# q and k of the fourth token chunk by seven block products, and a new plan for the splitting of the MLP's weights

## The chip, the cores and the metric

The kernel runs on one core of one Trainium2 chip. The metric is the time of one execution in device microseconds (us), as the median of several executions of the same program. TensorE (PE in the profile) does the matrix products, VectorE (DVE) sums, differences and reductions, ScalarE (ACT) copies and activations, GpSimd (POOL) elementwise products, and SyncE (SP) issues the transfers between DRAM and the on-chip memory (SBUF). PSUM is the memory of eight banks that TensorE writes its products to. Each engine runs its own list of instructions in the order of the program; engines wait for one another on semaphores.

## What is computed

The input x has S = 2048 tokens of D = 448 numbers. Two branches are mixed by a gate:

```python
qkv = x @ wqkv                     # q, k, v: 16 heads of 28 each
idx = pos - off * 2                # every token sees 8 tokens: itself, 2 back, 4 back ... 14 back
a = softmax(q . k[idx] / sqrt(28)) @ v[idx] @ wo
r = relu(x @ w1 + b1)              # w1: 448 x 1792
b = (r * r) @ w2 + b2              # w2: 1792 x 448
g = sigmoid(sum(x * gate_w))
out = g * a + (1 - g) * b
```

All of it is in fp32.

## The kernel before

**Precision.** TensorE is fed with a reduced form of fp32 (fp32r). Every operand is split into a high part (`h`: a copy by ACT that rounds) and a low part (`l`: raw minus high, by DVE), and each product is three passes: high by high, high by low, low by high. So every weight and every block of x costs two instructions beside the matmuls, one on ACT and one behind it on DVE: this is `split_full` (lines 129 to 132, the low part `LO_DELAY` later). A second way, `split_copied` (line 739), has ACT make the high part and a copy of the raw tile in one PSUM bank, the `copy_tile`, and has DVE subtract from that copy. There is one such bank at a time, so the next copy waits until the low part before it is made.

**Pairs.** The contraction of 448 is 3 x 128 + 64. Most matmuls have 64 rows of contraction, and two of them run next to each other on the lower and the upper half of TensorE's rows (`LOW`, `HIGH`): a pair, issued by `side_by_side` (line 194) or `beside` (line 349). After its first products a bank changes over to the other half of the rows; between the two DVE writes one element of the bank (`turn`, line 205; `turned`, line 358), and TensorE waits for that one-element memset. PSUM has two rings of four banks, tags `b` and `m`; a bank is taken anew when the reads of the tile that had it before are over.

**Stages.** The tokens are four chunks of 512, each four tiles of 128. Chunk 0 is `qkv_first`. Chunks 1 and 2 are `qkv_seven` (line 441): for each of the two pairs of tiles (a `Group`) q and k of two tiles, four blocks, are made of seven products with sums of tokens and sums of weights in place of eight; the seven accumulate in four banks per group named x, y, z, w. ACT carries a bank into a staging tile (`copied`), and DVE adds later banks to it (`added`); a full staging tile is stored to DRAM (`q_d`, `k_d`). v of two tiles at a time is a class `V`: `first`, a memset on each bank, `second`. The token sums are made by DVE in the raw x tile (lines 969 and 970) and split by ACT and DVE (`sums_begin`, line 1047). Chunk 3 is two calls of `qkv_two` (line 309), which makes q, k and v by plain products, 63 pairs a call; into the second are put the MLP's first products (`mlp_one`, `mlp_two`). In the listing below `xm[3]` is a copy of the chunk's x tiles for the MLP, made by three ACT instructions of 128x1024 (lines 1014 and 1088).

Behind this the MLP runs from chunk 3 on: h = x @ w1 by ACT and DVE into high and low parts, then the products with w2 (`b`). Beside them run attention (POOL's products `qk` and `av`, DVE's reductions of them, ACT's exponentials) by a unit of one token parity and one group of heads, and then the products with wo (`a`).

**Order of the work.** The code is a single stream in which TensorE's instructions come in order and `advance` moves a model clock on by each pair. `when(t, fn)` and `at(dt, fn)` put other engines' work into the program when that clock passes a time (in ns). So the position of an instruction on ACT, DVE, POOL and SP is set by these times and not by the chip. The four pieces of w1 (`w1_piece`, line 755) and the two first ones of w2 (`w2_piece`, line 790) are loaded into one of two raw tiles, which the raw x of chunks 0, 1 and 3 use too: a load waits until the tile's last reader is done. k = 3 of a w1 piece is the 64-row rest, which goes to `w17h` and `w17l` in four instructions.

Of the kernel before, what the change touches and what calls it, by code (L numbers as in the profile page):

```python
# [14 lines left out]
P = 128  # L15
# [3 lines left out]
G = 4  # L19
# [38 lines left out]
def gated_mix_kernel(ctx: ExitStack, tc: tile.TileContext, xT, wqkv, w1, w2, wo, b1, b2, out):  # L58
# [36 lines left out]

        return w1a[n][:, k], w1b[n][k]

    def w1_second():
        for n in range(2):
            for k in range(3):  # L100
                w1b[n][k] = halfp.tile([P, FA], F32R, tag=f"e{3 * n + k}", name=f"w1b{'hl'[n]}{k}")

    def w1_f(n, k, f):
        one, two = w1_rows(n, k)
# [268 lines left out]
    class Group:  # L373
# [52 lines left out]

        def stage(self, b):
            if self.st[b] is None:
                self.st[b] = stage_tile(f"st{self.c}_{self.u}_{b}", self.u > b and "e5")
            return self.st[b]  # L430

        def copied(self, n, b, r):
# [5 lines left out]
            if store:  # L438
                stage_store(st, self.c // 2, (self.c % 2) * 4 + 2 * self.u, b)

    def qkv_seven(c, x, inners):
# [19 lines left out]
        v = V(c, x, (0, 1), inners[0])  # L461
        v.first()
        first(1)
        v.second()
# [19 lines left out]
        v.first()  # L484
# [7 lines left out]
        v.second()  # L492

    class V:

# [14 lines left out]
        def second(self):  # L510
            beside(*(self.prods(i, rows, range(3)) for i, rows in ((1, LOW), (0, HIGH))))
# [240 lines left out]
            copy[1] -= 1  # L752
        when(t + COPY_DELAY, lows)

    def w1_piece(i, dt, gap):

        n = F // 4
        raw = raw_tile(f"w1raw{i}")
        nc.sync.dma_start(raw[:, :, :n], w1[i])
        sl = slice(i % 2 * n, (i % 2 + 1) * n)  # L760
        later_on = soon if i < 3 else lambda fn: at(1000.0, fn)

        def part(k, t):
            if i == 2 and k == 0:
                w1_second()
            if k < 3:
                hi, lo = (w1_rows(m, k)[i // 2][:, sl] for m in range(2))
            if k < 3 and i == 2:
                split_copied(t, raw[:, k, :n], [(slice(0, P), slice(0, n), hi, lo)])
                return  # L770
            if k < 3:
                split_full(raw[:, k, :n], hi, lo, later_on)
                return
            parts = []
            for a in range(i * n, i * n + n, 64):
                f, b = divmod(a, P)
                if b and a > i * n:
                    continue
                m = min(P - b, i * n + n - a)
                rows, o = slice(f % 2 * 64, f % 2 * 64 + 64), f // 2 * P + b  # L780
                parts.append((rows, slice(a - i * n, a - i * n + m), w17h[rows, o:o + m], w17l[rows, o:o + m]))
            if i == 2:
                split_copied(t, raw[:, 3, :n], parts)
                return
            for rows, cols, hi, lo in parts:
                split_full(raw[rows, 3, cols], hi, lo, later_on)
        for step, k in enumerate((0, 1, 3, 2) if i == 2 else range(4)):
            when(dt + step * gap, part, k, dt + step * gap)

    def w2_piece(i0, n, t, gap):  # L790
        raw = raw_tile(f"w2raw{i0}")
        nc.sync.dma_start(raw[:, :n, :D], w2[:, i0:i0 + n])
        for k in range(n):
            when(t + k * gap, lambda k: split_copied(t + k * gap, raw[:, k, :D], [
                (slice(0, P), slice(0, D), w2ah[:, i0 + k], w2al[:, i0 + k])]), k)

    def x_load(c):
        if c == 2:
# [134 lines left out]

    tw7 = xpool.tile([P, 2, CH], F32R, tag="x2", name="tw7")
    tw8 = halfp.tile([P, FA], F32R, tag="e4", name="tw8")
    w7x = tw7[:, 0, :D], tw7[:, 1, :D]
    for i, key in enumerate((n, half) for half in (False, True) for n in (1, 2, 3, 4)):
        wsum[key] = (w2ah[:, i], w2al[:, i]) if i < NFA else (tw8[:, :D], tw8[:, D:])  # L940

    def weight_sums():
# [13 lines left out]
        cuts += [lambda: split_full(o, *w7x, soon)]  # L956
        return one, two, cuts, [cut((1, True), q2), cut((2, True), z), cut((4, True), m), cut((3, True), k2)]


    def token_sums(c):  # L960
# [11 lines left out]
        def begin():  # L972
            if c == 1:
                t = [xpool.tile([P, 2 * CH], F32R, tag=f"x{n}", name=f"s{c}_0{'hl'[n]}")[:, 48:48 + CH + 2 * P] for n in range(2)]
                sums[c, 0] = [[v[:, :CH] for v in t], [v[:, CH:] for v in t]]
                t = attp.tile([P, 48 + 2 * (CH + 2 * P)], F32R, tag="v", name=f"s{c}_1")[:, 48:]
                t = [t[:, n * (CH + 2 * P):(n + 1) * (CH + 2 * P)] for n in range(2)]
                sums[c, 1] = [[v[:, :CH] for v in t], [v[:, CH:] for v in t]]
                return
            for j in range(2):  # L980
                t = [halfp.tile([P, FA], F32R, tag=f"e{2 * j + n}", name=f"s{c}_{j}{'hl'[n]}")[:, 48:48 + CH + 2 * P]
# [24 lines left out]
            return  # L1006
        xs[c] = X(own + [xpool.tile([P, 2, CH], F32R, tag="x3", name=f"x{c}_3")])

    xm3 = []

    def x_copy(c, j):

        xm3.append(xpool.tile([P, 2, CH], F32R, tag=f"x{j}", name=f"x{c}_{j}"))
        nc.scalar.activation(xm3[j], f32(xs[c].t[j]), AF.Copy)

    def x_more(c):
        xraw[c] = x_load(c)
# [15 lines left out]
    steps(13600.0, 700.0, cuts)  # L1033
    steps(16300.0, 700.0, two[:5])
    steps(24600.0, 300.0, two[5:])
    steps(27000.0, 0.0, more[:1])
    steps(30500.0, 900.0, more[1:])
    for c, t in SPLIT_AT.items():
        when(t, x_begin, c)
        for k in range(4):  # L1040
# [13 lines left out]
    when(25000.0, w1_piece, 0, 38400.0, 1500.0)  # L1054
# [4 lines left out]
    for j in range(2):  # L1059
        when(63700.0 + j * 2000.0, x_copy, 3, j)  # L1060
    when(85000.0, biases)
    when(81000.0, w2_piece, 0, 4, 90000.0, 1350.0)
    when(87400.0, w2_piece, 4, 3, 99000.0, 1350.0)

    pair = {}

    def mlp_one():
        pair[0] = h_first(xm[3], ORDER[0], 0)
        h_turn(pair[0], 0)

    def mlp_two():
        h_second(xm[3], pair[0], 0)
        ops = mlp_ops(pair[0], ORDER[0], 0, (HL_DELAY, HL_DELAY))
        emit(ops[:4])
        pair[1] = h_first(xm[3], ORDER[0], 2)
        h_turn(pair[1], 2)
        emit(ops[4:])

# [8 lines left out]
    xm[3] = X(xm3 + [xpool.tile([P, 2, CH], F32R, tag="x2", name="x3_2"), xs[3].t[3]])  # L1087
    at(2000.0, lambda: nc.scalar.activation(xm[3].t[2], f32(xs[3].t[2]), AF.Copy))
    x = xs[3]
# [417 lines left out]
```

## Time and profile before

| what | value |
|---|---|
| median of 3 runs | 411.77 us (411.44 to 411.81) |
| the profiled execution's own time | 411.63 us |
| its span in the trace | 409.9 us |
| TensorE busy | 404.7 us, 3799 matmuls |
| DVE, ACT, POOL busy | 288.2, 219.4, 267.5 us |

The span runs from the first instruction to the last that the profiler saw; 1.7 us of the run lie around it. In the profile an instruction is named by its line and its tiles, output first, buffer numbers left out. Rows of a timeline join neighbours of one kind: start, duration, engine, line, operation, tiles, shape, how many, and in brackets how long the engine sat idle before it and what released it. Line numbers of the profile are those of the listing above.

### The profile page before, as it was taken

Reading aid. Unit: us, or ns where it says so; the run is one execution under the profiler, and the core shown is the slowest. Engines: PE = TensorE matmul, PEld = TensorE weight load, DVE = VectorE, ACT = ScalarE, POOL = GpSimd, SP = SyncE. Lnnn points to the kernel's source line nnn. Section 1 sums busy time; section 2 is a strip of 40 time slices with the busy share of each in tenths; the row PEclk is TensorE's granted clock in tenths of the full one; section 3 lists DMA queues with packets and bytes.
Section 4 is the critical chain, followed back from the end, with each engine's and each line's share of the span. In section 5 each row is a group of like instructions: output and inputs, shape, how many; then the busy total and the mean of one; then the engine's idle time right before and its main releaser. Section 6 shows DMA issues by size and latency. Waiting matters only on the chain.

```text
span 409.9 us, 9374 instructions
## 1 busy us (share of the span) xinstructions
PE 404.7 (99%) x3799; PEld 362.8 (89%) x3799; DVE 288.2 (70%) x480; ACT 219.4 (54%) x498; POOL 267.5 (65%) x167
## 2 busy tenths in 40 slices
PE   8999999999999999999999999999999999999996
PEld 6999999999988888888888888988898888888996
DVE  4897884577659666686765898778776677784344
ACT  4758577376775465355565345354553254346640
POOL 0000000965999999979997899898989978950000
PEclk9999999999999999999999999999999999999999
DMA  7998999989281614454113649765236530048504
GB/s 226 354 359 259 349 372 259 367 274 315 91 296 43 209 58 150 185 188 153 39 47 130 199 146 260 221 146 159 55 127 217 203 130 0 32 124 174 125 3 179
DMA packets 67548, 73.99 MB, mean 181 GB/s; under 512 B 34544, under 2 KB 59824, under 8 KB 67376
## 3 DMA queue, kind: packets, MB, share of 16 engines
q1 hardware_dynamic: 67504, 73.39, 56.3%
q8 instruction: 29, 0.48, 0.5%
q14 instruction: 15, 0.12, 0.1%
HBM read 45.94 MB, written 28.25 MB: 181 GB/s over the span
## 4 chain that ended last, share of the span: by engine, by line
PE 97%; DMA 1%; SPq 0%; DVE 0%; ACT 0%; issue 0%
PE b L202 33%; PE h L202 33%; PE qkv L202 11%; PE a L202 7%; PE v L344 4%; PE x L344 3%; PE z L344 2%; PE qkv L291 1%; DMA xraw<-xT 1%; PE y L344 1%; PE w L344 1%; PE a L1279 1%; PE last L1279 0%; SPq L891 0%; SPq L886 0%; DVE bt L1158 0%
## 5 line engine op out<-in xcount | busy, mean ns | idle before, releaser
L561 POOL TENSOR_TENSOR qk<-q,k 128x896 f32<-128x896 f32 x64 | 134.8, 2147 | 84.4 <-DMA k<-k_d 77.3
L568 POOL TENSOR_TENSOR av<-lg,v 128x896 f32<-128x896 f32 x64 | 119.2, 1981 | 4.7 <-DVE lg L562 4.5
L866 DVE TENSOR_TENSOR h<-h,h 128x512 fp32r<-128x512 f32 x56 | 38.5, 689 | 58.5 <-ACT h L869 58.1
L562 DVE TENSOR_REDUCE lg<-qk 128x32 f32<-128x896 f32 x64 | 67.1, 1074 | 0.4 <-POOL qk L561 0.4
L576 DVE TENSOR_REDUCE o<-av 128x112 f32<-128x896 f32 x64 | 66.6, 1071 | 0.3 <-POOL av L568 0.3
L202 PE MATMUL b<-w2ah,h 64*128 64x448 f32 x448 | 66.3, 359 | 0.0
L202 PE MATMUL b<-w2bh,h 64*128 64x448 f32 x448 | 66.1, 359 | 0.0
L867 ACT ACTIVATE h<-h,b1z 128x512 f32<-128x512 f32 x56 | 36.7, 656 | 42.1 <-PE h L202 42.1
L202 PEld LDWEIGHTS b<-w2bh,h 64*128 64x128 f32 x448 | 42.0, 184 | 3.6
L202 PEld LDWEIGHTS b<-w2ah,h 64*128 64x128 f32 x448 | 41.9, 184 | 3.7
L202 PE MATMUL b<-w2bl,h 64*128 64x448 f32 x224 | 40.6, 358 | 0.0
L202 PE MATMUL b<-w2al,h 64*128 64x448 f32 x224 | 40.5, 358 | 0.0
L202 PE MATMUL qkv<-wqh,x 64*128 64x448 f32 (+1 forms) x240 | 36.1, 361 | 0.0
L868 ACT ACTIVATE h<-h 128x512 fp32r<-128x512 f32 x56 | 33.6, 599 | 1.7
L869 ACT ACTIVATE h<-h 128x512 f32<-128x512 f32 x56 | 33.3, 594 | 0.0
L814 ACT ACTIVATE h<-h 128x4 fp32r<-128x4 f32 (+1 forms) x35 | 7.2, 207 | 43.7 <-PE b L202 41.4
L202 PEld LDWEIGHTS qkv<-wqh,x 64*128 64x128 f32 x240 | 22.8, 185 | 1.5
L202 PEld LDWEIGHTS b<-w2bl,h 64*128 64x128 f32 x224 | 21.0, 184 | 1.9
L202 PEld LDWEIGHTS b<-w2al,h 64*128 64x128 f32 x224 | 20.9, 184 | 2.0
L202 PE MATMUL qkv<-wql,x 64*128 64x448 f32 (+1 forms) x120 | 21.9, 361 | 0.0
L243 ACT ACTIVATE st<-qkv 128x448 f32<-128x448 f32 x24 | 12.1, 543 | 9.9 <-PE qkv L202 9.1
L202 PE MATMUL h<-x,w1ah 64*128 64x512 f32 x84 | 16.5, 387 | 0.0
(280 smaller groups left out, 892.5 us busy)
## 6 DMA issues: line engine op xcount, KB each, us to landing
k<-k_d SPq DMA_DIRECT2D x8, 840.0 KB, 6.3
v<-v_d SPq DMA_DIRECT2D x8, 840.0 KB, 4.8
x_d<-x SPq DMA_DIRECT2D x12, 512.0 KB, 8.8
q_d<-st SPq DMA_DIRECT2D x8, 448.0 KB, 6.1
k_d<-st SPq DMA_DIRECT2D x8, 448.0 KB, 7.4
w1raw<-w SPq DMA_DIRECT2D x4, 896.0 KB, 13.4
q<-q_d SPq DMA_DIRECT2D x8, 448.0 KB, 3.7
o_d<-o SPq DMA_DIRECT2D x16, 224.0 KB, 2.2
```

Of the source, the lines that this page charges most:

```text
L202: nc.tensor.matmul(acc.pt[:, :acc.n], a[rows], w[rows], start=acc.todo == acc.all, stop=acc.todo == 1)
L243: nc.scalar.activation(st[:, :, t % 2], heads(pt), AF.Copy)
L344: nc.tensor.matmul(self.pt[:, :self.n], a, w, start=new, stop=True, skip_group_check=True)
L561: nc.gpsimd.tensor_mul(pr, q[:, s:s + 1].to_broadcast([P, W, C]), k[:, s:s + W])
L562: pending.append(lambda: nc.vector.tensor_reduce(lg[:, s], pr.rearrange("p w (h d) -> p w h d", h=HG), axis=AX.X, op=ALU.add))
L568: nc.gpsimd.tensor_mul(pr.rearrange("p (h d) w -> p w h d", h=HG), lg[:, s][:, :, :, None].to_broadcast([P, W, HG, DH]), v[:, s:s + W].rea ...
L576: nc.vector.tensor_reduce(o[:, g * C:(g + 1) * C], pr, axis=AX.X, op=ALU.add)
L814: nc.scalar.activation(ap, f32(ap), AF.Copy)
L866: nc.vector.tensor_sub(hl, pt, f32(hh))
L867: ops += [lambda pt=pt, r=r: nc.scalar.activation(pt, pt, AF.Relu, bias=b1t[:, f + r:f + r + 1]), lambda pt=pt, hh=hh: nc.scalar.activatio ...
L868: lambda pt=pt, hh=hh: nc.scalar.activation(hh, pt, AF.Square),
L869: lambda pt=pt, r=r, low=low: (nc.scalar.activation(pt, pt, AF.Square), at(delays[r], low))]
```

## The change

Chunk 3 goes through `qkv_seven` too. It has no v at its start; its v tiles 0 and 1 follow q and k as in the other chunks, and tiles 2 and 3 come last, with the MLP's first products put into their second half. For that the token sums of chunk 3 are made in its raw tile (which the load of the third w1 piece takes over) and split by ACT and DVE during chunk 2. Two further edits hold for chunks 1 and 2 as well:

- the end of `qkv_seven` has another order. Before: v first, product 7 second half, ACT's copies, DVE's adds of w, product 3, DVE's adds of z, the rest of product 7, DVE's adds of x, v second. After: ACT's copies of w, product 3, adds of z, product 7 second half, adds of x, v first, the rest of product 7 into the same x banks, adds of x, v second.
- in chunks 2 and 3 the `copy_tile` bank is taken between the first halves of the products, and in chunk 3 again between v first and v second of tiles 2 and 3.

The weights' splits are replanned. The second w1 piece goes through the copy bank, later; the third is split in two halves around chunk 3's q and k; the fourth has its high parts made by ACT early, and its low parts by POOL. The three copies of x by ACT become three transfers from SBUF to SBUF on SP's queue. w2's pieces are loaded later: the first takes the raw tile of the fourth w1 piece, so it waits for POOL's low parts.

```diff
+            if c == 3:
+                t = [xpool.tile([P, 2 * CH], F32R, tag=f"x{i}", name=f"s3_{i}") for i in range(3)]
...
         first(4)
+        if copies:
+            copy_tile()
...
         other(4, 1, 0)
-        v = V(c, x, (2, 3), inners[1])
-        v.first()
-        second(7)
-        each("copied", 7, 0, 1)
-        each("added", 4, 0, 1, True)
+        each("copied", 4, 0, 1)
         first(3, False)
         each("added", 3, 1, 0)
+        second(7)
+        each("added", 7, 0, 1, True)
+        v = V(c, x, (0, 1) if beside_v else (2, 3), inners[1])
+        v.first()
         other(7, 1, 1)
         each("added", 7, 1, 1, True)
         v.second()
+        if beside_v:
+            v = V(c, x, (2, 3), inners[0])
+            v.first()
+            copy_tile()
+            v.second(beside_v)
...
+                nc.scalar.activation(hi, raw[rows, k, cols], AF.Copy)
...
+                    nc.gpsimd.tensor_sub(lo, raw[rows, k, cols], f32(hi))
...
+    when(56500.0, sums_begin, 3, 56600.0, 800.0, 59900.0, 1100.0)
...
-    when(45700.0, w1_piece, 1, 56200.0, 1300.0)
-    when(65000.0, w1_piece, 2, 74500.0, 1400.0)
-    when(66000.0, w1_piece, 3, 83700.0, 900.0)
...
+    when(45700.0, w1_piece, 1, [(k, 62700.0 + k * 1350.0) for k in range(4)])
+    when(65000.0, w1_piece, 2, [(3, 69600.0), (0, 71000.0), (2, 82400.0), (1, 83800.0)])
...
-    qkv_seven(2, xs[2], ("pp", (own_v, b2t)))
...
-    qkv_two(x, 3, 0, copies=True)
-    qkv_two(x, 3, 2, (mlp_one, mlp_two), True)
+    qkv_seven(2, xs[2], ("pp", (own_v, b2t)), True)
+    when(88000.0, x_copies)
+    qkv_seven(3, xs[3], (None, None), True, (mlp_one, mlp_two))
+    h_second(xs[3], pair[1], 2)
```

Three places show what the change moves. The first is DVE at the end of chunk 1, before: `w17l` is the 64-row rest of w1, `st1` are staging tiles, `w1`, `z1`, `x1` with two more numbers are banks of chunk 1, and `v1_2`, `v1_3` the banks of v's tiles 2 and 3.

```order
L970 TENSOR_TENSOR xraw2_2_497<-xraw2_3_498,xraw2_2_497 128x2x128
L970 TENSOR_TENSOR xraw2_3_498<-xraw2_3_498,xraw2_2_497 128x2x128
L131 TENSOR_TENSOR w17l_73<-w1raw0_531,w17h_72 64x128 x3
L131 TENSOR_TENSOR w17l_73<-w1raw0_531,w17h_72 64x64
L360 MEMSET v1_2_813 1x1
L360 MEMSET v1_3_815 1x1
L437 TENSOR_TENSOR st1_0_0_656<-w1_0_732,st1_0_0_656 128x4x112
L437 TENSOR_TENSOR st1_1_0_658<-w1_1_734,st1_1_0_658 128x4x112
L437 TENSOR_TENSOR st1_0_1_714<-z1_0_660,st1_0_1_714 128x4x112
L437 TENSOR_TENSOR st1_1_1_716<-z1_1_662,st1_1_1_716 128x4x112
L437 TENSOR_TENSOR st1_0_1_714<-x1_0_580,st1_0_1_714 128x4x112
L437 TENSOR_TENSOR st1_1_1_716<-x1_1_582,st1_1_1_716 128x4x112
```

And the same place after:

```order
L994 TENSOR_TENSOR xraw2_2_496<-xraw2_3_497,xraw2_2_496 128x2x128
L994 TENSOR_TENSOR xraw2_3_497<-xraw2_3_497,xraw2_2_496 128x2x128
L441 TENSOR_TENSOR st1_0_1_713<-z1_0_659,st1_0_1_713 128x4x112
L441 TENSOR_TENSOR st1_1_1_715<-z1_1_661,st1_1_1_715 128x4x112
L441 TENSOR_TENSOR st1_0_0_655<-x1_0_579,st1_0_0_655 128x4x112
L441 TENSOR_TENSOR st1_1_0_657<-x1_1_581,st1_1_0_657 128x4x112
L130 TENSOR_TENSOR w17l_73<-w1raw0_530,w17h_72 64x128 x3
L130 TENSOR_TENSOR w17l_73<-w1raw0_530,w17h_72 64x64
L359 MEMSET v1_2_847 1x1
L359 MEMSET v1_3_849 1x1
L441 TENSOR_TENSOR st1_0_1_713<-x1_0_579,st1_0_1_713 128x4x112
L441 TENSOR_TENSOR st1_1_1_715<-x1_1_581,st1_1_1_715 128x4x112
```

Before, four low parts (`w17l`) and v's memsets came ahead of all six adds. After, four adds (z, then x) come ahead of the `w17l` and of v's memsets, and x's bank is used again behind them.

The second place is ACT in the last third of chunk 2, before: `st2` are staging tiles, `x2`, `z2`, `w2` banks of chunk 2, `w1ah` and `w17h` high parts of the second w1 piece.

```order
L433 ACTIVATE st2_0_0_1041<-x2_0_968 128x4x112
L433 ACTIVATE st2_1_0_1043<-x2_1_970 128x4x112
L130 ACTIVATE w1ah_70<-w1raw1_872 128x448 x2
L433 ACTIVATE st2_0_1_1085<-z2_0_1045 128x4x112
L433 ACTIVATE st2_1_1_1087<-z2_1_1047 128x4x112
L130 ACTIVATE w17h_72<-w1raw1_872 64x64
L130 ACTIVATE w17h_72<-w1raw1_872 64x128 x3
L433 ACTIVATE st2_0_1_1085<-x2_0_968 128x4x112
L433 ACTIVATE st2_1_1_1087<-x2_1_970 128x4x112
```

And after:

```order
L437 ACTIVATE st2_0_1_1087<-z2_0_1045 128x4x112
L437 ACTIVATE st2_1_1_1089<-z2_1_1047 128x4x112
L129 ACTIVATE s3_1_1098<-xraw3_667 128x512
L129 ACTIVATE s3_2_1099<-xraw3_667 64x256 x2
L129 ACTIVATE s3_0_1097<-xraw3_667 128x512
L129 ACTIVATE s3_2_1099<-xraw3_667 64x256 x2
L764 ACTIVATE w1ah_70<-w1raw1_871 128x448
L765 ACTIVATE copy14_1133<-w1raw1_871 128x448
L437 ACTIVATE st2_0_1_1087<-x2_0_967 128x4x112
L437 ACTIVATE st2_1_1_1089<-x2_1_969 128x4x112
```

The splits of chunk 3's token sums (`s3_1`, `s3_0`, `s3_2`) stand between the copies of z and the copies of x; the last x copies (product 7) have become copies of w (product 4).

The third is POOL at the change from the first attention unit (`qk0`) to the second (`qk1`), before:

```order
L561 TENSOR_TENSOR qk0_6_1383<-q00_923,k00_924 128x896
L561 TENSOR_TENSOR qk0_7_1415<-q00_923,k00_924 128x896
L561 TENSOR_TENSOR qk1_0_1558<-q01_1442,k01_1443 128x896
L561 TENSOR_TENSOR qk1_1_1610<-q01_1442,k01_1443 128x896
L561 TENSOR_TENSOR qk1_2_1621<-q01_1442,k01_1443 128x896
```

And after:

```order
L580 TENSOR_TENSOR qk0_6_1414<-q00_922,k00_923 128x896
L580 TENSOR_TENSOR qk0_7_1443<-q00_922,k00_923 128x896
L805 TENSOR_TENSOR w1bl0_1255<-w1raw3_1230,w1bh0_1252 128x448
L805 TENSOR_TENSOR w1bl2_1256<-w1raw3_1230,w1bh2_1254 128x448
L805 TENSOR_TENSOR w17l_73<-w1raw3_1230,w17h_72 64x64
L805 TENSOR_TENSOR w17l_73<-w1raw3_1230,w17h_72 64x128 x3
L805 TENSOR_TENSOR w1bl1_1467<-w1raw3_1230,w1bh1_1253 128x448
L580 TENSOR_TENSOR qk1_0_1598<-q01_1485,k01_1486 128x896
L580 TENSOR_TENSOR qk1_1_1627<-q01_1485,k01_1486 128x896
L580 TENSOR_TENSOR qk1_2_1662<-q01_1485,k01_1486 128x896
```

Seven low parts of the fourth w1 piece (`w1raw3`) stand between the two units. The raw tile that they read is the one that the first w2 piece is loaded to.

More of the change, by code (lines that the diff above doesn't have):

```diff
@@ L96, in w1_rows, with w1_second @@
         return w1a[n][:, k], w1b[n][k]
[L98 to L101, printed above, removed]
+    def w1_second(*which):
+        for n, k in which:
+            w1b[n][k] = halfp.tile([P, FA], F32R, tag=f"e{3 * n + k}", name=f"w1b{'hl'[n]}{k}")
     def w1_f(n, k, f):
@@ L508, in first, with second @@
             turned(*self.banks)
-        def second(self):
-            beside(*(self.prods(i, rows, range(3)) for i, rows in ((1, LOW), (0, HIGH))))
+        def second(self, between=()):
+            todo = [self.prods(i, rows, range(3)) for i, rows in ((1, LOW), (0, HIGH))]
+            a = 0
+            for fn in between:
+                fn()
+                beside(*((bank, prods[a:a + 3]) for bank, prods in todo))
+                a += 3
+            beside(*((bank, prods[a:]) for bank, prods in todo))
             for i, (bank, tl) in enumerate(zip(self.banks, self.tls)):
@@ L753, in split_copied, with w1_piece @@
         when(t + COPY_DELAY, lows)
-    def w1_piece(i, dt, gap):
+    def w1_piece(i, order, later_on=None):
         n = F // 4
@@ L760, in w1_piece @@
         sl = slice(i % 2 * n, (i % 2 + 1) * n)
-        later_on = soon if i < 3 else lambda fn: at(1000.0, fn)
         def part(k, t):
-            if i == 2 and k == 0:
-                w1_second()
             if k < 3:
[L767 to L783, printed above, removed]
+                hi, lo = (w1_rows(m, k)[i // 2][:, sl] if w1_rows(m, k)[i // 2] is not None else None for m in range(2))
@@ new lines, in part @@
+                parts = [(slice(0, P), slice(0, n), hi, lo)]
+            else:
+                parts = []
+                for a in range(i * n, i * n + n, 64):
+                    f, b = divmod(a, P)
+                    if b and a > i * n:
+                        continue
+                    m = min(P - b, i * n + n - a)
+                    rows, o = slice(f % 2 * 64, f % 2 * 64 + 64), f // 2 * P + b
+                    parts.append((rows, slice(a - i * n, a - i * n + m), w17h[rows, o:o + m], w17l[rows, o:o + m]))
@@ L784, in part, with low @@
+            if i in (1, 2):
+                split_copied(t, raw[:, k, :n], parts)
                 return
             for rows, cols, hi, lo in parts:
[L786 to L790, printed above, removed]
+                if i < 3:
+                    split_full(raw[rows, k, cols], hi, lo, soon)
+                    continue
+                nc.scalar.activation(hi, raw[rows, k, cols], AF.Copy)
+                def low(rows=rows, cols=cols, hi=hi):
+                    lo = w1_rows(1, k)[1][:, sl] if k < 3 else w17l[rows, hi_cols[id(hi)]]
+                    nc.gpsimd.tensor_sub(lo, raw[rows, k, cols], f32(hi))
+                if k == 3:
+                    a = i * n + cols.start
+                    f, b = divmod(a, P)
+                    o = f // 2 * P + b
+                    hi_cols[id(hi)] = slice(o, o + cols.stop - cols.start)
+                when(later_on[k], low)
@@ L791, in w2_piece @@
+        hi_cols = {}
+        for k, t in order:
+            when(t, part, k, t)
+    def w2_piece(i0, n, order):
         raw = raw_tile(f"w2raw{i0}")
         nc.sync.dma_start(raw[:, :n, :D], w2[:, i0:i0 + n])
-        for k in range(n):
-            when(t + k * gap, lambda k: split_copied(t + k * gap, raw[:, k, :D], [
-                (slice(0, P), slice(0, D), w2ah[:, i0 + k], w2al[:, i0 + k])]), k)
+        for k, t in order:
+            when(t, lambda k, t: split_copied(t, raw[:, k, :D], [
+                (slice(0, P), slice(0, D), w2ah[:, i0 + k], w2al[:, i0 + k])]), k, t)
```

72 lines of the change are left out of this document (41 added, 31 removed).

## The prediction

> **What bounds the kernel now.** I read the page first, then the timelines of PE, DVE, ACT and SP from 44 to 110 us. Of the page: the span, busy time by engine, PE's 40 slices and granted clock, and the chain that ended last.
>
> ```profile
> span 409.9 us, 9374 instructions
> PE 404.7 (99%) x3799; PEld 362.8 (89%) x3799; DVE 288.2 (70%) x480; ACT 219.4 (54%) x498; POOL 267.5 (65%) x167
> PE   8999999999999999999999999999999999999996
> PEclk9999999999999999999999999999999999999999
> PE 97%; DMA 1%; SPq 0%; DVE 0%; ACT 0%; issue 0%
> ```
>
> PE is busy all the time at full clock. So every pair taken away is time gained, and every new wait of PE is time lost: no slack lies elsewhere to take it up. A change of 0.2% (0.8 us) or less can't be told from none.
>
> **The products saved.** The order lists 18 matmuls fewer, nine pairs. PE's timeline in chunk 2 gives a pair's price:
>
> ```profile
> 70.39 0.36 PE L344 MATMUL x<-w2ah,s_0h 64*128 64x448 f32 x2
> 72.19 0.36 PE L344 MATMUL v<-wqh,x 64*128 64x450 f32 x2
> 74.67 0.37 PE L344 MATMUL x<-w2ah,s_0h 64*128 64x448 f32 x2
> 76.51 0.48 PE L344 MATMUL x<-wqh,x 64*128 64x448 f32 x2
> 79.03 0.36 PE L202 MATMUL qkv<-wqh,x 64*128 64x448 f32 x2
> ```
>
> From 70.39 to 72.19 there are nine pairs: 0.200 each, so the change gains **1.80 us**. v's first half, 12 pairs, takes 74.67 - 72.19 = 2.48.
>
> **The end of chunk 1.** PE there, before:
>
> ```profile
> 48.37 0.36 PE L344 MATMUL v<-wqh,x 64*128 64x450 f32 x2
> 50.84 0.36 PE L344 MATMUL x<-w2ah,s_0h 64*128 64x448 f32 x2
> 51.44 0.36 PE L344 MATMUL z<-wqh,s 64*128 64x448 f32 x2
> 52.68 0.47 PE L344 MATMUL x<-wqh,x 64*128 64x448 f32 x2
> 53.39 0.36 PE L344 MATMUL v<-wqh,x 64*128 64x450 f32 x2
> ```
>
> And DVE beside it:
>
> ```profile
> 50.30 0.88 DVE L970 TENSOR_TENSOR xraw<-xraw,xraw 128x256 f32<-128x256 f32 x2
> 51.09 1.17 DVE L131 TENSOR_TENSOR w17l<-w1raw,w17h 64x128 fp32r<-64x128 f32 x4
> 52.26 0.06 DVE L360 MEMSET v<- 1x1 f32 x2
> 52.37 1.16 DVE L437 TENSOR_TENSOR st<-w,st 128x448 f32<-128x448 f32 x2
> 53.44 1.15 DVE L437 TENSOR_TENSOR st<-z,st 128x448 f32<-128x448 f32 x2
> ```
>
> DVE is back to back and free for the next thing at 51.09. In the new order PE does z (six pairs, to 49.57), x's second half (to 50.17), v's first half (to 52.65), and then comes back to the x banks, which DVE must have added by then. DVE's adds of z and x start at 51.09 and take 1.07 a pair of adds (52.37 to 53.44): done at 53.23. With about 0.05 for the signal PE waits **0.63**. Behind the adds stand the `w17l`, 1.17, and v's memsets, 0.11: 54.5. PE would begin v's second half at 53.3 + 0.6 = 53.9 and waits **0.6**. Before, PE lost 0.15 at this place (52.68 for 52.64, and 0.47 for 0.36). Net +1.1. The adds that left the tail only make DVE idle later.
>
> **Chunk 2**, with PE 1.1 later. ACT's trio of splits, ACT's copies of z, its `w17h`, and two of DVE's rows:
>
> ```profile
> 52.65 1.38 ACT L130 ACTIVATE s_1h<-xraw 128x512 fp32r<-128x512 f32 x3
> 65.80 1.02 ACT L433 ACTIVATE st<-z 128x448 f32<-128x448 f32 x2
> 66.83 1.26 ACT L130 ACTIVATE w17h<-w1raw 64x64 fp32r<-64x64 f32 x4
> 77.12 1.08 DVE L562 TENSOR_REDUCE lg<-qk 128x32 f32<-128x896 f32 x1
> ```
>
> The copies of z start at 65.7 + 1.1 = 66.8 at the earliest and take 1.0. Two trios of the new token sums follow (2 x 1.38), a high part and a copy for w1 (1.0 for two 128x448 by the z row), then the copies of x (1.0): 72.5. PE wants the x banks at 70.39 + 1.1 = 71.5 and waits **1.0**. It then ends product 4 at 72.19 + 2.1 = 74.3. ACT copies w (1.0), makes `w17h` (1.26) and its copy (0.5): 77.1. DVE's low parts take 1.17 and the adds of x 1.07: 79.3. PE is back at x at 74.3 + 1.2 + 0.6 + 2.48 = 78.6 and waits **0.75**. Next on DVE is a reduction of attention, 1.0, ahead of v's memsets: 80.4, against 79.35 + 0.6 = 79.95 on PE: **0.45**. Before, 0.15 was lost here too (76.51). Net +2.05; chunk 3 starts at 79.03 + 3.15 = 82.2.
>
> **Loads of w1 in chunk 3.** Rows of SP, of the page's DMA list, of ACT, and busy time by window (stretch, sum, then PE, PEld, DVE, ACT, POOL, granted clock, DMA share, GB/s):
>
> ```profile
> 68.78 1.32 SPq L759 DMA_DIRECT2D w1raw<-w  x2
> w1raw<-w SPq DMA_DIRECT2D x4, 896.0 KB, 13.4
> 80.49 0.58 ACT L745 ACTIVATE w1bh<-w1raw 128x448 fp32r<-128x448 f32 x1 [0.15 <-DMA w1raw<-w]
> 62.00:64.00 2.00, 2.00 (x24) 1.87 (x21) 0.78 (x3) 0.71 (x4) 0.00 (x0) 1.00 1.14 320
> 70.00:72.00 2.00, 2.00 (x24) 1.87 (x22) 0.14 (x4) 1.67 (x2) 0.81 (x1) 1.00 0.75 143
> 74.00:76.00 2.00, 2.00 (x23) 1.86 (x22) 0.09 (x2) 0.53 (x2) 2.00 (x2) 1.00 1.05 391
> ```
>
> The third piece now waits for DVE's low parts of the token sums and is issued near 72 (in the 2.76 of trios above, from 67.8, plus a low part or two). Before, two pieces issued at 68.78 shared the queue, and the first took 11.6 us (to 80.4). Alone, at the 391 GB/s of 74 to 76, its 896 KB would take 2.3. I take half of 11.6, since the fourth piece now comes some 5 us behind: 77.8. Product 2 of chunk 3 takes the copy bank 1.2 after the start, at 83.4; two rounds stand before that (1.26, 0.5, 1.17, 0.5, 0.55 and some signals), so the piece is wanted by about 79. Bounds: no wait at 2.3, and 83.6 less 78.9, 4.7, at 11.6. I take 0, as 77.8 is in time.
>
> The fourth, issued near 77.3 when the second piece's last low part is made, is wanted at ACT by 85: its high parts (1.0 and 1.26) stand ahead of ACT's first copies of x (1.0), and PE wants that x again 30 pairs after 82.2, at 88.2. At 5.8 there is no wait, at 13.4 one of 5.7. I take 0: its 896 KB and the two q stores (448 KB each, issued by then) are 1.8 MB, 4.7 us at 391 GB/s, and some 2 more until it lands make 84.
>
> The token sums' own work (by L970 eight times 0.44, and six low parts by the rate of the trio, 3 us) comes to DVE between 60 and 72, where the windows leave it 1.2 and 1.9 of 2 us, and w1's second piece leaves that stretch; I take nothing. ACT's three copies of x go, 3 us in which it had nothing to do for PE: nothing gained.
>
> **v's last tiles in chunk 3.** POOL, ACT, DVE, SP:
>
> ```profile
> 78.36 10.48 POOL L561 TENSOR_TENSOR qk<-q,k 128x896 f32<-128x896 f32 x5 [0.89 <-DMA v_d<-st]
> L1321 POOL TENSOR_TENSOR w2bl<-w2raw,w2bh 128x448 fp32r<-128x448 f32 x2 | 2.3, 1170 | 0.5 <-ACT w2bh L1320 0.5
> L599 POOL TENSOR_TENSOR lg<-lg,mask 128x256 f32<-128x256 f32 x8 | 5.5, 686 | 1.4 <-DVE lg L562 1.4
> 86.98 0.38 SPq L792 DMA_DIRECT2D w2raw<-w  x1
> 94.20 0.58 ACT L745 ACTIVATE w2ah<-w2raw 128x448 fp32r<-128x448 f32 x1
> v<-v_d SPq DMA_DIRECT2D x8, 840.0 KB, 4.8
> 95.55 0.64 DVE L751 TENSOR_TENSOR w2al<-copy,w2ah 128x448 fp32r<-128x448 f32 x1
> 96.91 0.62 DVE L751 TENSOR_TENSOR w2al<-copy,w2ah 128x448 fp32r<-128x448 f32 x1
> ```
>
> Two low parts of w2 must leave the copy bank before v's tile 3 can have it. The first w2 piece is loaded into the raw tile of w1's fourth, whose low parts POOL makes behind its last `qk0`. That product ended at 88.84; with the reductions that free its buffers behind more adds I put it at 90. Three low parts of 1.17 and four small ones (between 0 and 0.69, taken 0.4) make 95.1. The load, issued at 86.98 before and in hand by 94.20, took 7.2 at most; a k or v of 840 KB takes 4.8. I take 6: 101.2. A high part, a copy and a low part, and a second round, 1.36 by the DVE rows, add 2.9: 104.1. PE comes there 96 pairs after 82.2, at 101.7, and waits **2.4**. With the load at 4.8 or 7.2 it would be 1.2 or 3.6; if the data were there early DVE would still have its memsets, a reduction, the adds of x and two rounds between 99.2 and 103.1: not under **1.4**.
>
> [...]
>
> POOL's low parts relieve DVE of some 3 us that lay under PE's work, so nothing is gained by it.
>
> [...]
>
> **Behind it** come the second w2 piece and the chain of h. SP and ACT before:
>
> ```profile
> 95.12 0.78 SPq L792 DMA_DIRECT2D w2raw<-w  x1
> 105.13 0.56 ACT L745 ACTIVATE w2ah<-w2raw 128x448 fp32r<-128x448 f32 x1
> ```
>
> Between issue and use lay 10 us. Now SP has the three x transfers ahead of it, and they wait until product 7 has read the token sums' tiles, 84 pairs after 82.2: 99. The piece lands 4.8 to 7.2 later, at 105 to 107, and ACT, with its first h behind it, wants it at 105.1 + 3.15 - 1.8 + 2.4 = 108.9: in time by 2 us. For DVE's low parts of h, which stand behind two more w2 rounds, and ACT's touches I take 0.5 between 0 and 1. On SP the second unit's q and k now pass the first w2 piece, which waits for POOL anyway. The tail has nothing new.
>
> Sum on the profiled run: 411.63 - 1.80 + 1.1 + 2.05 + 2.4 + 0.5 = 415.9; it lies 0.14 under the median, so the forecast is **416.0**.
>
> **The rivals.**
> - *Faster: the waits don't come about.* If DVE ends the adds of x by 52.65 in chunk 1, and ACT and DVE keep up likewise in chunk 2, only the nine pairs count, and the load of w2 is early: 411.77 - 1.8 = 410.0. For it: DVE's and ACT's mean use is 70% and 54%. Against: the rows from 50.30 to 54.5 leave no gap on DVE, and the work ahead is 0.6 us too long. It decides whether DVE can start the adds before 50.5; it can't unless the sums of x (L970) run sooner. Chance 0.10.
> - *Only chunks 1 and 2 wait.* w2 is there early and DVE's reductions fall elsewhere: -1.8 + 3.15 + 0.2: 413.3. Chance 0.2.
> - *The loads are late too.* w1's third piece lands at 81 to 83, or the fourth after 87, as the full queue before suggests (11.6 and 13.4): 2 to 5 more, 418 to 421, say 419. Chance 0.2.
> - *The change doesn't remove the pairs*: the program has 3771 rows for 3789 on PE. No chance.
>
> **How the numbers follow.** The forecast has 0.5, its own range 414.4 to 417.6 (1.4 for 2.4 and 0 for 0.5 below; 3.6 and 1 above). The 8-in-10 range leaves out the fast case and the worst of the late loads: 412.6 to 419.6. Faster by over 0.2%: 0.10; within: 0.05, out of the second rival's chance, for waits half as long; slower: 0.85.
>
> **What would show it.** In the new profile: PE's idle by DVE at L344 twice at the end of chunk 1 (x, then v), by ACT at product 7 and by DVE at x and v in chunk 2, and a wait of over 1.4 us at v's tile 3 in chunk 3; chunk 3 starting at 82 and taking 1.8 less beside its waits. I am wrong if PE has no wait over 0.3 in 50 to 82, or if its largest wait is for a transfer of w1.

## The result, and the profile after

The changed kernel takes **421.38 us** (median of 4 runs, 420.60 to 421.95); the kernel before, run beside it, 411.62 (411.44 to 411.81). The ratio is 1.0236, interval [1.0215, 1.0256]. It is slower, as forecast, but by 9.8 us where the forecast had 4.2, and beyond the range, which ended at 419.6. The profiled execution took 420.94, 9.31 more than the one before, and the trace below accounts for that.

The page after: span, busy times, PE's slices and granted clock, and the chain that ended last.

```profile
span 419.2 us, 9379 instructions
PE 406.7 (97%) x3781; PEld 361.5 (86%) x3781; DVE 298.6 (71%) x501; ACT 220.8 (53%) x505; POOL 273.9 (65%) x174
PE   8999999699799999999999999999999999999996
PEclk9999999999999999999999999999999999999999
PE 75%; DVE 6%; ACT 2%; DMA 1%; issue 1%; POOL 0%; DVEq 0%
```

The 18 matmuls are gone (3781 for 3799), but PE now has holes in its first third, and the chain leaves PE for DVE and ACT there. Its new waits of 0.4 and more, by engine and line, say for what (us in total, times, longest):

```profile
PE v L343 <- DVE w2al L770: 2.7, 1, 2.7
PE x L343 <- DVE st L441: 2.2, 2, 1.7
PE z L343 <- DVE z L359: 0.9, 1, 0.9
PE x L343 <- DVE x L359: 0.5, 1, 0.5
PE v L343 <- DVE v L359: 0.5, 2, 0.3
PE x L343 <- ACT st L437: 0.4, 1, 0.4
```

Five of the six rows are for DVE. PE's timeline gives their places, and in its rows without brackets the starts of stages: chunk 3 begins at 85.42, the first product `b` of the MLP at 122.35, the last product at 415.60.

```profile
52.95 0.47 PE L343 MATMUL x<-wqh,x 64*128 64x448 f32 x2 [0.56 <-DVE st L441]
54.10 0.47 PE L343 MATMUL v<-wqh,x 64*128 64x450 f32 x2 [0.28 <-DVE v L359]
...
71.68 0.90 PE L343 MATMUL x<-w2ah,s_0h 64*128 64x448 f32 x2 [0.43 <-ACT st L437]
75.12 0.49 PE L343 MATMUL z<-wqh,s_1h 64*128 64x448 f32 x2 [0.93 <-DVE z L359]
77.12 0.47 PE L343 MATMUL x<-w2ah,s_0h 64*128 64x448 f32 x2 [0.49 <-DVE x L359]
...
80.23 0.52 PE L343 MATMUL v<-w7h,x 64*128 64x450 f32 x2
82.41 0.47 PE L343 MATMUL x<-wqh,x 64*128 64x448 f32 x2 [1.66 <-DVE st L441]
82.72 0.36 PE L343 MATMUL x<-wql,x 64*128 64x448 f32 x2
83.49 0.48 PE L343 MATMUL v<-wqh,x 64*128 64x450 f32 x2 [0.21 <-DVE v L359]
85.42 0.36 PE L343 MATMUL x<-wqh,x 64*128 64x448 f32 x2
...
108.07 0.47 PE L343 MATMUL v<-wqh,x 64*128 64x450 f32 x1 [2.73 <-DVE w2al L770]
122.35 0.37 PE L201 MATMUL b<-w2ah,h 64*128 64x448 f32 x2
415.60 0.27 PE L1311 MATMUL last<-woh,o 128*128 128x224 f32 x1
```

The same two ends before:

```profile
114.10 0.37 PE L202 MATMUL b<-w2ah,h 64*128 64x448 f32 x2
406.44 0.27 PE L1279 MATMUL last<-woh,o 128*128 128x224 f32 x1
```

| stage | forecast, us | measured, us |
|---|---|---|
| start of chunk 1 | 0 | -0.4 (30.96 for 31.37) |
| chunk 1 | +1.1 | +1.2 (to 56.01, before to 55.24) |
| chunk 2, to the start of chunk 3 | +2.05 | +5.6 (85.42 - 56.01, less 79.03 - 55.24) |
| chunk 3, to the first `b` | -1.8 + 2.4 = +0.6 | +1.9 (122.35 - 85.42, less 114.10 - 79.03) |
| behind | +0.5 | +0.9 (415.60 - 122.35, less 406.44 - 114.10) |

So 3.6 of the surplus lies in chunk 2, 1.3 in chunk 3. A part of the second is a way of reading: a wait costs PE more than its bracket. From 80.23 to 82.72 are two steps of PE, 0.40 without a wait; they took 2.49, which is 2.09 lost, with 1.66 in the bracket. The rest is PE running empty (matmuls start 0.20 apart and last 0.36) and a first pair that holds the next up for 0.31. At the waits of chunks 1 and 2 this comes to 0.26 to 0.51 more than the bracket; at v's tile 3 the loss is 3.0 for 2.73.

What made DVE late in chunk 2 is one row of its timeline; POOL's and ACT's stand below it.

```profile
69.82 5.19 DVE L130 TENSOR_TENSOR s<-xraw,s 128x512 fp32r<-128x512 f32 x3
75.01 0.06 DVE L359 MEMSET z<- 1x1 f32 x2
...
70.36 8.70 POOL L580 TENSOR_TENSOR qk<-q,k 128x896 f32<-128x896 f32 x4 [68.97 <-DMA k<-k_d]
...
75.78 0.55 ACT L765 ACTIVATE copy<-w1raw 128x448 f32<-128x448 f32 x1 [3.25 <-DVE w1al L770]
```

Three low parts of the token sums take 5.19. By the source line's view, their durations run from 415 to 2326 ns:

```profile
L130 DVE TENSOR_TENSOR s<-xraw,s x6: 415/698/2326, 68.2 to 72.8; 64x256 fp32r<-64x256 f32 x4, 128x512 fp32r<-128x512 f32 x2
```

The 64x256 ones took 0.42 before POOL's first attention product began at 70.36, and 2.33 and 2.22 beside POOL's products; one such product takes 2.1. z's memset, which PE waits for, stands behind them, as do the low part that frees the copy bank (ACT stands still for 3.25) and the adds of x.

### The profile page after: what moved, and what is told of

It is laid out like the page before. It is cut to its first block, busy times and chain, and to the rows that moved or that the text cites. A ratio compares the mean times of both kernels' runs of the same rounds, so it can differ in the third digit from the quotient of the medians.

```text
span 419.2 us, 9379 instructions
## 1 busy us (share of the span) xinstructions
PE 406.7 (97%) x3781; PEld 361.5 (86%) x3781; DVE 298.6 (71%) x501; ACT 220.8 (53%) x505; POOL 273.9 (65%) x174
## 4 chain that ended last, share of the span: by engine, by line
PE 75%; DVE 6%; ACT 2%; DMA 1%; issue 1%; POOL 0%; DVEq 0%
PE b L201 32%; PE h L201 31%; PE a L201 7%; PE v L343 2%; DMA w2raw<-w 1%; DVE s L130 1%; PE x L343 1%; PE a L1311 1%; ACT copy L765 1%; DVE bt L1190 1%; PE y L343 1%; DVE st L441 1%; DVE x L130 0%; DVE o L595 0%; ACT st L437 0%
## 5 line engine op out<-in xcount | busy, mean ns | idle before, releaser
L343 PE MATMUL v<-wqh,x 64*128 64x450 f32 x144 | 23.9, 368 | 3.2 <-DVE w2al L770 2.7
L343 PEld LDWEIGHTS v<-wqh,x 64*128 64x128 f32 x144 | 15.5, 185 | 5.5 <-DVE w2al L770 3.1
L201 PE MATMUL h<-x1b,w1ah 64*128 64x512 f32 x84 | 16.1, 387 | 0.0
L201 PE MATMUL h<-x,w1bh 64*128 64x512 f32 x84 | 16.1, 386 | 0.0
```

Of the source, the lines that this page charges most:

```text
L201: nc.tensor.matmul(acc.pt[:, :acc.n], a[rows], w[rows], start=acc.todo == acc.all, stop=acc.todo == 1)
L343: nc.tensor.matmul(self.pt[:, :self.n], a, w, start=new, stop=True, skip_group_check=True)
```

## The experiments

**1. POOL waits.** Theory P: the low parts, with both inputs in SBUF, can't run while a product of POOL does. A one-column subtraction on POOL that reads the last of the low parts stands ahead of its first product:

```diff
+                if i == 0:
+                    lo = f32(sums[3, 0][1][1][:, P:P + 1])
+                    nc.gpsimd.tensor_sub(pool_wait, lo, lo)
                     yield piece(lambda: qk_piece(i, q, k, lgs[i], s), QK_COST if i else QK_FIRST)
```

> The changed kernel with one thing more: ahead of its first attention product POOL does a tiny subtraction that reads the last low part of chunk 3's token sums, so that no attention product runs beside those low parts; nothing else is moved. Theory P (a DVE subtraction with both sources in SBUF stands still while POOL multiplies): the two low parts of 64x256 fall from 2.2 to 2.3 us to 0.42 each, the three in a row from 5.19 to 1.5, PE's waits of 0.9 and 0.5 us for z and x memsets in chunk 2 go, the one of 1.7 for the adds of x falls to about 0.75, POOL starts about 1 us later, and the time falls by 3 to 4 us, to 417.5 to 418.5. Theory Q (DVE is only too full by the order of its list, and POOL plays no part): the low parts stay at 2.2, the time stays at 421 or rises by up to 1.

419.21 (417.77 to 420.40), ratio 1.0189 [1.0163, 1.0215]; the profiled run 418.75. DVE, POOL, SP and ACT there:

```profile
69.78 1.47 DVE L130 TENSOR_TENSOR s<-xraw,s 128x512 fp32r<-128x512 f32 x3
...
71.33 0.19 POOL L681 TENSOR_TENSOR pool_wait<-s 128x1 f32<-128x1 f32 x1 [69.94 <-DVE z L359]
71.49 8.35 POOL L580 TENSOR_TENSOR qk<-q,k 128x896 f32<-128x896 f32 x4
90.23 2.26 POOL L808 TENSOR_TENSOR w1bl<-w1raw,w1bh 128x448 fp32r<-128x448 f32 x2
...
71.28 6.14 SPq L781 DMA_DIRECT2D w1raw<-w  x2
95.64 0.39 SPq L821 DMA_DIRECT2D w2raw<-w  x1
...
101.59 0.58 ACT L767 ACTIVATE w2ah<-w2raw 128x448 fp32r<-128x448 f32 x1 [5.40 <-DMA w2raw<-w]
```

The three low parts take 1.47, the waits for z and x's memsets are gone, and chunk 3 starts at 82.12 (85.42 after). Chunk 2 is 3.2 shorter, so theory P holds for it; the run gained only 2.2, for the 3 to 4 expected. Chunk 3, to the first `b`, took 38.1 for 36.9. Why stands in the windows of this trace (stretch, length, then busy time and instructions of PE, PEld, DVE, ACT, POOL, then granted clock, DMA share, GB/s):

```profile
100.81:104.22 3.41, 1.31 (x13) 0.87 (x9) 1.85 (x4) 2.44 (x6) 2.48 (x2) 1.00 1.08 404
104.22:107.63 3.41, 3.08 (x16) 2.79 (x18) 2.26 (x3) 2.03 (x7) 2.06 (x2) 0.50 0.99 345
```

Behind the wait at v's tile 3 (2.43) PE runs at half its clock for 3.4 us, which costs some 1.5 here (chunk 3 is 1.2 longer than in the profile after, with a wait 0.3 shorter). In the profile after this stretch isn't there, but the other runs after show a granted clock of 0.995 and 0.996 as against its 0.998, and this kernel's 0.991 to 0.998. Single runs don't follow the clock alone: the fastest run after, 420.60, has 0.996.

**2. The same cost put into the kernel before.** There every low part of a weight that stands beside POOL's products takes a copy in PSUM. Here those of the copied splits take the raw tile:

```diff
-                nc.vector.tensor_sub(lo, pt[rows, cols], f32(hi))
+                nc.vector.tensor_sub(lo, raw[rows, cols], f32(hi))
```

> The kernel before, with the low parts of the copied splits subtracted from the raw tile in SBUF and not from its copy in PSUM; ACT still makes the copy. Same list of instructions on every engine. Theory P: each of these low parts that meets a product of POOL takes up to 2.6 us for 0.62, the four small ones together up to 8 for 1.13, and PE comes to wait for memsets and banks behind them: 3 to 10 us slower, 415 to 422. Theory Q: 0.61 to 0.64 each as before, and the time within 0.5 us of 411.7.

416.53 (416.13 to 417.17), ratio 1.0130 [1.0114, 1.0147]: 5.1 slower by one input's place. DVE's rows, and one of POOL's (its product before that ran from 70.04 to 80.51):

```profile
79.53 2.07 DVE L562 TENSOR_REDUCE lg<-qk 128x32 f32<-128x896 f32 x2
81.52 4.26 DVE L751 TENSOR_TENSOR w1bl<-w1raw,w1bh 128x448 fp32r<-128x448 f32 x2
...
86.89 3.11 DVE L751 TENSOR_TENSOR w17l<-w1raw,w17h 64x128 fp32r<-64x128 f32 x4
90.94 0.64 DVE L751 TENSOR_TENSOR w1bl<-w1raw,w1bh 128x448 fp32r<-128x448 f32 x1
...
80.69 4.60 POOL L561 TENSOR_TENSOR qk<-q,k 128x896 f32<-128x896 f32 x2 [0.18 <-DVE lg L562]
```

A low part of 0.61 to 0.63 from PSUM takes 2.1 from SBUF beside POOL's products (1.78 and 2.55), and 0.64 when POOL is idle; reductions (one input) go on at 1.07 beside POOL (the one at 76.42). Taken singly, each of the two low parts ends 0.5 behind the end of the product that it met (83.30 for 82.82, 85.78 for 85.29), as if it waited for that product; and the product that began meanwhile took 2.51. In the profile after, the two of 2.33 and 2.22 end 0.27 and 0.28 behind such a product (72.75 for 72.48, 75.00 for 74.72). So beside POOL's products the low parts with both inputs in SBUF were held up (1.78 and 2.55 against 0.64), and those with one of the two in PSUM (0.61 and 0.63 before) and the reductions (1.07) weren't.

**3. The new end order alone**, in chunks 1 and 2 of the kernel before:

```diff
-        v = V(c, x, (2, 3), inners[1])
-        v.first()
-        second(7)
-        each("copied", 7, 0, 1)
-        each("added", 4, 0, 1, True)
+        each("copied", 4, 0, 1)
         first(3, False)
         each("added", 3, 1, 0)
+        second(7)
+        each("added", 7, 0, 1, True)
+        v = V(c, x, (2, 3), inners[1])
+        v.first()
```

> The kernel before with only the new order of the end of the seven-product stage, for chunks 1 and 2; chunk 3 stays plain, no split is replanned. By the prediction's first step chunk 1 pays 1.1 us (PE waits 0.6 for the adds of x and 0.3 to 0.6 for v's memsets). In chunk 2 no token sums are split, DVE has little ahead of the adds, so 0 to 0.6 there. Sum 1.1 to 1.7, so 412.8 to 413.5. If the order costs nothing by itself and only the work put into chunk 2 does (rival): 411.5 to 412.0.

412.47 (412.09 to 414.73, 8 runs), ratio 1.0034 [1.0019, 1.0049]. Its waits:

```profile
PE x L344 <- DVE st L437: 0.6, 1, 0.6
PE v L344 <- DVE v L360: 0.3, 1, 0.3
```

Both lie in chunk 1 (at 53.02 and 54.19), which takes 1.1 more than before: this is the order's own cost. Chunk 2's waits aren't; with no new work on ACT and DVE the order costs nothing there (chunk 2 is 0.2 shorter than before), and so the time lies 0.3 below the expected band.

**4. Chunk 1 freed**: in the kernel after, two rounds of the first w1 piece are planned behind the adds.

```diff
-    when(25000.0, w1_piece, 0, [(k, 38400.0 + k * 1500.0) for k in range(4)])
+    when(25000.0, w1_piece, 0, [(0, 38400.0), (1, 39900.0), (2, 47500.0), (3, 48500.0)])
```

> The changed kernel with the last low part and the four small ones of the first w1 piece planned some 8 us later, behind chunk 1's last adds. DVE then starts the adds of z some 0.5 us sooner and v's memsets 1.7 sooner: PE's two waits at the end of chunk 1 (0.56 and 0.28, with the slower first pairs about 1.1 in all) fall to 0 to 0.2, and the time falls by 0.9 to 1.1 if nothing takes their place in chunk 2, by less if DVE's work of chunk 2 is late instead: 420.2 to 420.9.

418.89 (417.78 to 419.57), ratio 1.0180 [1.0159, 1.0201]: 2.5 less than after, not 0.9 to 1.1. Chunk 1's waits are gone, and the collision too, without its being touched:

```profile
69.47 1.47 DVE L130 TENSOR_TENSOR s<-xraw,s 128x512 fp32r<-128x512 f32 x3
...
71.63 8.35 POOL L580 TENSOR_TENSOR qk<-q,k 128x896 f32<-128x896 f32 x4 [70.24 <-DMA k<-k_d]
```

k came 1.3 later (71.63 for 70.36) and the low parts 0.35 earlier. The collision hangs on about 1 us between two engines that don't wait for each other. Here, too, v's tile 3 waits 2.7, and the clock falls behind it (0.50 in 106 to 108; 0.995 to 0.999 over the runs).

**5, 6 and 7. A wait by itself.** Does such a wait cost PE its clock? In the kernel before, DVE makes one low part of h 2, 4 or 6 times more (same values), ahead of chunk 1's first `b`:

```diff
+                for _ in range(more):
+                    nc.vector.tensor_sub(hl, pt, f32(hh))
                 nc.vector.tensor_sub(hl, pt, f32(hh))
```

> The kernel before, with one low part of h made three times over on DVE (2 x 0.68 us more, the same values) ahead of TensorE's first product of w2 with the second token chunk's h. Theory H (a wait of TensorE of some 2.4 us is already enough to bring the clock to half speed for a stretch of 3.41 us, as the profiles of the first and fourth experiment show behind v's tile 3; a short wait isn't): one wait of about 1.0 (1.35 less the 0.3 of slack), granted clock 0.999 or more in all runs, 412.4 to 413.0. Rival (the stretch at half speed belonged to something else in those kernels): the same here.

> As the kernel with two more low parts, but four more (2.7 us). A wait of about 2.4. Theory H: some or all runs show a granted clock of 0.996 to 0.998 and take up to 1.7 more (half of 3.41): 414 to 416, and its profile has a stretch of PEclk near 0.5 behind the wait. Rival: clock 0.999 or more, 413.8 to 414.4 in all runs.

> Six more low parts (4.1 us), a wait of about 3.8. Theory H: half clock in every run, 416.5 to 417.3, clock 0.996 or below. Rival: 415.2 to 415.8 at 0.999 or more. If only this one and not the one with four shows half clock, the bound lies between 2.4 and 3.8 us.

Before beside them: 411.32 (15 runs, 410.79 to 413.94). With two more: 412.30 (411.76 to 413.50), ratio 1.0012 [0.9993, 1.0032], clock 0.998 to 1.000 in ten runs. With four: 415.58 (413.65 to 416.12), ratio 1.0082 [1.0054, 1.0111], in two groups: 413.65 and 414.01 at 0.999; 415.40, 415.75 and 416.12 at 0.994 (and one of 415.92 at 1.000, which the clock doesn't explain; before has two such runs, 413.64 and 413.94 at 1.000). With six: 417.06 (416.45 to 417.71), ratio 1.0125 [1.0086, 1.0165], all four at 0.995 or 0.996. PE's row behind the wait, with two more:

```profile
247.12 0.67 PE L202 MATMUL b<-w2ah,h 64*128 64x448 f32 x4 [0.76 <-DVE h L868]
```

With four, and a window of that trace:

```profile
248.05 1.06 PE L202 MATMUL b<-w2ah,h 64*128 64x448 f32 x4 [2.20 <-DVE h L868]
```

```profile
248.15:251.56 3.41, 3.41 (x20) 3.06 (x22) 3.41 (x6) 0.00 (x0) 1.36 (x1) 0.50 0.81 221
```

With six:

```profile
250.22 1.11 PE L202 MATMUL b<-w2ah,h 64*128 64x448 f32 x4 [3.65 <-DVE h L868]
```

Theory H holds: with nothing else changed, a wait of 0.8 leaves the clock alone in ten runs, one of 2.2 brings it to half in three of six by their clock, one of 3.7 in all four. The price is the 1.9 between the two groups (1.5 by their spans), near half of 3.41.

The traces also show what may let a wait of one size do it in some runs only. The clock on record in the traces of before and after has one stretch at 1.00 each, from 4.53 to 410.72 and from 4.67 to 417.68: 119 and 121 times 3.413 us. Each half-clock stretch behind a wait follows 3.41 us in which PE was idle for 2.1 (first experiment: 3.41 less the 1.31 busy), 2.7 (fourth), 2.2 (with four more) or 3.1 (with six). In the profile after, the place 30 times 3.413 behind 4.67, at 107.07, cuts the wait of 2.73 in two, with 1.73 idle ahead of it (3.41 less 1.68) and 1.00 behind, and the clock stays:

```profile
103.66:107.07 3.41, 1.68 (x17) 1.20 (x13) 1.86 (x4) 1.77 (x4) 2.12 (x1) 1.00 1.07 395
```

At the end of the same trace the clock falls, behind 3.41 us with 1.81 idle (3.41 less 1.60):

```profile
414.27:417.68 3.41, 1.60 (x15) 1.42 (x13) 1.23 (x3) 0.00 (x0) 0.00 (x0) 1.00 0.49 175
417.68:419.16 1.48, 0.00 (x0) 0.00 (x0) 0.00 (x0) 0.00 (x0) 0.00 (x0) 0.50 0.00 0
```

The second experiment has a wait of 2.15 (at 91.14), in a profiled run with a clock of 1.000. So in these traces the fall goes with the idle time in one such stretch (1.81 and more, against 1.73 without a fall) and not with the length of the wait alone (2.20 with, 2.73 without), by matmul ends that the profile models. That a wait of 2.2 did it in half of the runs would then come from where the stretches lie against it; this is my estimate from those numbers, and no run tests it by itself.

**8. POOL's low parts back on DVE**, on top of the first experiment:

```diff
-                    nc.gpsimd.tensor_sub(lo, raw[rows, k, cols], f32(hi))
+                    nc.vector.tensor_sub(lo, raw[rows, k, cols], f32(hi))
```

> The first experiment's kernel (POOL's first product waits for the token sums' low parts), with the fourth w1 piece's low parts on DVE instead of POOL. Theory L (v's tile 3 waits for the load of w2, which waits for POOL's low parts): the low parts are made between 88 and 93 on DVE, one of them up to 2.2 us long where it stands beside a product of POOL; the load is issued at 92 to 94 and not at 95.6; the wait at v's tile 3 falls from 2.43 to between 0.8 and 1.9, but w's memsets behind the low parts may cost 0 to 1. Total 417.5 to 419.5; with the wait under 2 us the clock should be 0.998 or more in every run. Rival (DVE's own queue holds tile 3 up, not the load): the wait stays at 2.3 or more.

417.55 (417.10 to 418.22), ratio 1.0139 [1.0107, 1.0172]; clock 0.998 or 0.999 in all four runs. DVE, SP and PE there:

```profile
91.97 1.16 DVE L808 TENSOR_TENSOR w1bl<-w1raw,w1bh 128x448 fp32r<-128x448 f32 x2
102.40 1.15 DVE L441 TENSOR_TENSOR st<-x,st 128x448 f32<-128x448 f32 x2
103.47 0.62 DVE L773 TENSOR_TENSOR w2al<-copy,w2ah 128x448 fp32r<-128x448 f32 x1
...
94.92 0.39 SPq L821 DMA_DIRECT2D w2raw<-w  x1
...
94.29 0.47 PE L343 MATMUL w<-w2ah,x 64*128 64x448 f32 x2 [0.56 <-DVE w L359]
105.37 0.47 PE L343 MATMUL v<-wqh,x 64*128 64x450 f32 x1 [1.39 <-DVE w2al L773]
```

The wait at v's tile 3 falls to 1.39. What is left is DVE's own queue, since the w2 low part now stands right behind the adds of x; so of the 2.43 about 1.0 was the load's, which POOL's low parts held up. I missed the times: the low parts came later than expected, in a gap of POOL, and none was held up; the load went out only 0.7 earlier, and was in hand 1.9 earlier (99.69 for 101.59). PE gained nothing there: waits of 0.28 (bank y, at 84.22) and 0.56 (the w row) came up, and from the start of chunk 3 to the end of the wait lie 23.0 (82.38 to 105.37) for 22.4 in the first experiment (82.12 to 104.55). The 1.7 gained on the first experiment goes with the stretch at half clock, which no run shows here.

**9. Chunk 1's order set back as well:**

```diff
+        if c == 1:
+            v = V(c, x, (2, 3), inners[1])
+            v.first()
+            second(7)
+            each("copied", 7, 0, 1)
+            each("added", 4, 0, 1, True)
+            first(3, False)
+            each("added", 3, 1, 0)
+        else:
```

> The kernel with the low parts on DVE, with the end order of chunk 1 set back as well (v first, then product 7, w, product 3). Theory (the waits add up): the 0.56 at x and 0.28 at v in chunk 1 go, chunk 1 costs 1.1 less, the rest stays as in the eighth experiment: 417.55 - 1.1 = 416.45, between 416.0 and 416.9. Rival (DVE and ACT, 1.1 earlier against the loads, wait the time away again in chunk 2): 417.2 to 417.8, with longer waits in chunk 2.

416.85 (416.18 to 416.89), ratio 1.0103 [1.0055, 1.0151] to a before of 411.80: inside the expected band, at its upper end; chunk 3 starts 1.3 earlier than in the eighth (81.04 for 82.38), of which 0.4 lies ahead of chunk 1. This is the fastest form with the nine pairs saved. No form that beat the kernel before was found.

## Why the prediction was right or wrong

- **The failed step** is chunk 2's, in the words on record: "The token sums' own work [...] comes to DVE between 60 and 72 [...]; I take nothing." I asked whether DVE had time for it and not what ran beside it. POOL's first product, held up by k, falls into that stretch, and two low parts waited a product each: 2 x 1.85 = 3.7, and chunk 2 lost 3.6 more than forecast. Experiments 1 and 2 show it both ways. Without the collision chunk 3 starts at 82.12, where the forecast had 82.2; that it comes so close is in part luck. Chunk 1 began 0.6 earlier than before (30.80 for 31.37), and chunks 1 and 2 cost 3.7 for 3.15: chunk 2's waits were shorter than forecast (0.42, 0.70 and 0.20 for 1.0, 0.75 and 0.45), but each cost 0.3 to 0.5 more than its bracket.
- **DVE beside POOL** had no term in the forecast's sum. The trace of before had a hint that I read past: every low part of a weight beside POOL's products took its input from a copy in PSUM (0.61 and 0.63 for 128x448), at the price of a copy by ACT.
- **The nine pairs**: they are gone, and nothing speaks against the 1.8, though no run shows it alone. Chunk 3 changed by +1.9, of which 3.0 are the wait at v. The other 0.7 isn't a wait: some 0.4 is spacing (pairs with 448, 450 and 512 columns start 0.203, 0.207 and 0.233 apart, before 0.201, 0.203 and 0.229), some 0.2 two slow steps (0.34 at 113.86 and at 120.15). Why, no run shows.
- **Chunk 1**: right, in place and size (1.2; 1.1 in the third experiment); the waits were shorter than forecast (0.56 and 0.28 for 0.63 and 0.6), and each cost 0.27 more than its bracket.
- **w1's loads**: right for the changed kernel, with a margin smaller than forecast. With the collision the third piece was issued at 75, and PE waited for neither; without it (first experiment), at 71.3 for the 72 forecast, and ACT had it at 77.8. In the fourth and eighth experiment it took 8.3 and 8.2 for the 5.8 taken (in hand at 79.30 and 79.76), and PE then waited 0.19 and 0.28 at bank y for the copy bank; in the ninth 0.43.
- **v's tile 3**: the mechanism was right, and in the first experiment, where chunk 3 starts as forecast, so were the steps: POOL's low parts from 90.23 (forecast 90), the load issued at 95.64 (95.1) and used at 101.59 (101.2), the wait 2.43 (2.4). The load took 5.95 at most, near the 6 taken (4.77 in the eighth). In the eighth the floor of 1.4 came out as 1.39. The price was short twice: by some 0.3 for an emptied PE, and by 1.5 to 1.9 where the clock fell.
- **Behind**: 0.9 for 0.5, within its bounds; the one wait that the trace lists there is for DVE's low part of h, as forecast, but only 0.2 long.
- **The rivals**: the one with late loads had 419, near the result, but by another mechanism, and the largest wait was for no w1 transfer. None held the collision or the fall of the clock, and so the range ended too low.

The ninth form still spans 5.2 more than before (415.1). Its brackets in chunks 2 and 3 sum to 3.7; six waits of an emptied PE make some 2 more, the part behind chunk 3 0.8, the pairs take 1.8 off, and chunk 1 starting 0.8 earlier than before (30.56 for 31.37) as much again: 3.9. The last 1.3 stays open; some 0.5 of it is the wider spacing of chunk 3's pairs, which this trace shows too.

## What to carry to other kernels

Before an elementwise instruction is moved on DVE, look at where its two inputs lie and at what GpSimd does at that time: here two inputs in SBUF beside GpSimd products of 2.1 us cost up to 1.9 us each (2.33 for 0.42, 2.55 for 0.64), however idle DVE is on average (71% busy). When a kernel makes copies that seem needless, as the copy bank's here, ask what they avoid. Price a wait of a TensorE as busy as this one as the bracket plus 0.3 to 0.5 (0.26 to 0.51 here), and where it comes to 2.2 us or more, add the risk of a stretch at half clock, which cost 1.5 to 1.9 here.

## What the runs showed of the hardware that was not expected

- A 64x256 subtraction of 0.42 us took 2.2 and 2.3, and a 128x448 one of 0.62 took 1.8 and 2.5, beside GpSimd products of 2.1; the products lost little (8.70 for 8.35 in four).
- A TensorE wait of 2.2 us was enough for a stretch of 3.4 us at a granted clock of 0.50, in three of six runs by the clock; one of 0.8 in none of ten, one of 3.7 in all four. In the profile after it stayed at 1.00 behind 3.41 us with 1.73 of them idle, inside a wait of 2.73, and fell behind 3.41 us with 1.81 idle. A kernel with a wait of 2.2 us or more can spread: 417.8 to 420.4 in the first experiment, where the kernel before stayed within 0.9 on the same chip. A spread alone doesn't show it: on another chip the kernel before ran from 410.79 to 413.94 at 0.999 or more.
